# First batch's decays in two parts, corrections in one operation, and chunk magnitudes as powers of two

## The chip, the cores and the metric

The kernel runs on one core of a Trainium2 chip. Its engines are TensorE (PE, matrix multiply), VectorE (DVE), ScalarE (ACT), GpSimd (POOL) and SyncE (SP), each with its own queue of instructions, worked in order. The metric is the device time of one execution in microseconds. Times that belong to one profiled execution are counted from its first instruction.

## The reference

The layer takes q, k, v and a complex decay a (4 batches, 8 heads, 768 positions, 48 numbers a head), carries a state through the positions, and sends the result through two mixers:

```python
mag = np.sqrt(a_re * a_re + a_im * a_im)
scale = np.minimum(mag, 0.999) / (mag + 1e-06)
a_re_n, a_im_n = (a_re * scale, a_im * scale)
for t in range(S):
    ar, ai = (a_re_n[:, :, t, :, None], a_im_n[:, :, t, :, None])
    new_re = ar * S_re - ai * S_im
    new_im = ar * S_im + ai * S_re
    kv = np.einsum('bhd,bhe->bhde', k[:, :, t], v[:, :, t])
    S_re, S_im = (new_re + kv, new_im)
    y[:, :, t] = np.einsum('bhd,bhde->bhe', q[:, :, t], S_re)
# x: y with the heads side by side, 384 numbers a position
h = np.maximum(xt @ w_tok1, 0.0) @ w_tok2        # xt: positions last
u = x + h.transpose(0, 2, 1)
x = u + np.maximum(u @ w_ch1, 0.0) @ w_ch2
xn = (x - mu) / np.sqrt(var + 1e-06) * g_ln
out = x + np.maximum(xn @ w_ch1, 0.0) @ w_ch2    # second set of weights
```

## The kernel before

The recurrence is turned into products. The running product of the decays up to each position multiplies q, and its inverse multiplies k; within a chunk of 128 positions the result is then a masked matrix product, and a small scan over the six chunks carries the state. Four generators issue this, and a scheduler sets each engine's order from what they issue.

`gen_E` makes the decays and the products of one batch, on rows of 128 (head, number) pairs: 384 such rows are three row tiles, i = 0, 1, 2, each in two halves `hf` of 384 positions. It has four stages. **A** loads a into the tile `aj` (`load_a`), squares it (L202), and normalises it (L207 to L226). **The scan** (L228 to L230) multiplies 16 blocks of 24 columns one after the other, 15 complex steps (`cmul`) over all three row tiles at once. **L2** (L231 to L272) scans the 24 column ends in a tile `I`, takes the chunks' magnitudes by ScalarE (L248, L249) and a Newton step, and makes one correction for each column in the tile `C`. **C** (L273 to L343) goes by row tile and half: two products of `aj` with the correction (L295, L297, to `t`), a difference and a sum into `aj` (L299, L301), which read every third number; squares, logarithm and exponential for the inverse; the products with q and k (L328, L330); and DMAs on SP that put them into a tile `stk` for each head (L337, L338). Heads 0 and 1 lie in row tile 0; head 2 in 0 and 1; 3 and 4 in 1; 5 in 1 and 2; 6 and 7 in 2.

`gen_P` works one head on PE: transposes of k (L415), scores (L428) which VectorE masks (L433), state products (L455) and the chunk scan on VectorE (L456), the output (L475 to L487), and its split into two 16-bit halves `xh` and `xl` (L384). When the v of head 7 is loaded it also issues the second batch's three loads of a (L364 to L367). `gen_W` splits a weight tile that came as 64-bit numbers into two 16-bit halves by three operations on VectorE and one on ScalarE (L520 to L524); 4 token weights and 24 channel weights. `gen_M` is the two mixers: token products (L597 to L616), and hidden tiles (`relu_split`, L563 on ScalarE and L565 on VectorE), 198 in all.

In the first batch all loads are pieces of 4 runs of 192 numbers (L60). SP's queue holds, in order: the six loads of a, the constants, gl, q and k, weights, v, and then the transfers to `stk`. `gstat`, a product of gl with itself (L95), stands early in VectorE's queue.

Of the kernel before, what the change touches and what calls it, by code (L numbers as in the profile page):

```python
# [9 lines left out]
F32 = mybir.dt.float32  # L10
# [11 lines left out]
P = 128  # L22
# [14 lines left out]
def tile_kernel(ctx: ExitStack, tc: tile.TileContext, a_in, qk_in, v_in, aq2_in, v2_in, wt_in, wm1_in, wm2_in, w64_in, g_in, c_in, out):  # L37
# [16 lines left out]
    def steps(x, i, half):  # L54

        x = x.rearrange("p x (h i s) -> p (x h) i s", i=3, h=2)[:, :, i]
        return x if half is None else x[:, :, half * (HB // 2):(half + 1) * (HB // 2)]

    def load_a(b, i, half=None):
        nc.sync.dma_start(out=steps(aj, i, half), in_=steps(a_in[b], i, half))  # L60

    for half in range(2):
        for i in range(3):
            load_a(0, i, half)
# [123 lines left out]
    def gen_E():  # L188
# [3 lines left out]
        av = aj.rearrange("p x (j k r) -> p x j k r", j=6, k=KB)  # L192
        for b in range(B):
            rec[0] = b == 0
            for hf in range(2):
                for i in range(3):
                    ah = steps(aj, i, hf)
                    t = scratch(b, 2 * i + hf)
                    s4, s5, s6, s7 = (t[:, j * HB:(j + 1) * HB] for j in range(4))
                    g = wact.get(min(27, AG + (2 * i + hf) * AGS)) if b == 1 and AG >= 0 else None  # L200
                    with (tc.issue_after(g) if g is not None else ExitStack()):
                        A.activation(out=t[:, 0:2 * HB].rearrange("p (y s) -> p y s", y=4), in_=ah, func=AF.Square)  # L202
                    yield "wait"
                    if b < PNA:
                        nn = pe_sum(PNT, (eye, s4), (eye, s5))
                    else:
                        V.scalar_tensor_tensor(out=s4, in0=s4, scalar=TINY, in1=s5, op0=ALU.add, op1=ALU.add)  # L207
                        nn = s4
                    A.activation(out=s5, in_=nn, func=AF.Ln, bias=b_tiny if b < PNA else b_zero)
                    A.activation(out=s5, in_=s5, func=AF.Exp, scale=-0.5, bias=b_ln)  # L210
                    A.activation(out=s6, in_=s5, func=AF.Square, scale=1.0 / 0.4995,
                                 accum_out=rstat[:, 6 * b + 2 * i + hf:6 * b + 2 * i + hf + 1])
                    if b == 0:
                        V.tensor_scalar(out=s7, in0=s5, scalar1=-EPS / 0.4995, scalar2=1.0, op0=ALU.mult, op1=ALU.add)
                    else:
                        A.activation(out=s7, in_=s5, func=AF.Identity, scale=-EPS / 0.4995, bias=b_one)
                    yield 470
                    yield "wait"
                    V.scalar_tensor_tensor(out=s4, in0=nn, scalar=-1.0, in1=s6, op0=ALU.mult, op1=ALU.mult)
                    yield 470  # L220
                    V.scalar_tensor_tensor(out=s5, in0=s4, scalar=3.0, in1=s5, op0=ALU.add, op1=ALU.mult)
                    yield 470
                    V.scalar_tensor_tensor(out=s4, in0=s5, scalar=1.0, in1=s7, op0=ALU.min, op1=ALU.mult)
                    yield 470
                    ah = ah.rearrange("p (x h) s -> p x h s", x=2)
                    V.tensor_tensor(out=ah, in0=ah, in1=pair(s4.rearrange("p (h s) -> p h s", h=2)), op=ALU.mult)  # L226
                    yield 870
                for j in range(max(1, hf * KB // 2), (hf + 1) * KB // 2):  # L228
                    cmul(av[:, 0, :, j], av[:, 1, :, j], av[:, :, :, j], av[:, :, :, j - 1], [6, 24])
                    yield 1200  # L230
            yield "L2"  # L231
            NC3 = 3 * NCH
            I = ap.tile([P, 2, 6, 24], F32, tag="I", name="I")
            Iv = I.rearrange("p x (i h) r -> p x i h r", i=3)
            for h in range(2):
                V.tensor_copy(out=Iv[:, :, :, h], in_=av[:, :, 3 * h:3 * h + 3, KB - 1])
            yield 400
            for d in (3, 6, 12):
                cmul(I[:, 0, :, d:], I[:, 1, :, d:], I[:, :, :, d:], I[:, :, :, :24 - d], [6, 24 - d])
                yield 900  # L240
            ac = I[:, :, :, 21:24]
            sq = ap.tile([P, 2, NC3], F32, tag="sq", name="sq")
            st = ap.tile([P, 4, NC3], F32, tag="st", name="st")
            r0, r1, r2, dc = (st[:, j] for j in range(4))
            pc = pstat[:, b]
            V.tensor_tensor(out=sq.rearrange("p x (h c) -> p x h c", c=3), in0=ac, in1=ac, op=ALU.mult)
            V.scalar_tensor_tensor(out=pc, in0=sq[:, 0], scalar=TINY, in1=sq[:, 1], op0=ALU.add, op1=ALU.add)
            A.activation(out=r0, in_=pc, func=AF.Ln)  # L248
            A.activation(out=r0, in_=r0, func=AF.Exp, scale=-0.5)  # L249
            yield 300  # L250
# [23 lines left out]
            for i in range(3):  # L274
# [66 lines left out]
                if b and b + 1 < B:  # L341
                    load_a(b + 1, i)
# [810 lines left out]
```

## Time and profile before

| | us |
|---|---|
| runs | 962.79, 964.20, 966.58 (median 964.2) |
| span of the profiled execution | 960.0 |
| PE busy / VectorE busy / ScalarE busy | 816.3 / 746.6 / 495.8 |
| mean granted PE clock, share of full | 0.973 |

The page gives a span and not a whole time for the profiled execution; the median of the runs is 4.2 us above the span. Busy counts the time in which an engine worked on something, so PE's 816.3 us are 85% of the span and VectorE's 78%. A row of the time order gives start, length, engine, line, operation, what it writes and reads, shapes, count, and in brackets how long the engine sat idle before it and what ended that.

### The profile page before, as it was taken

Reading aid. Unit: us, or ns where it says so; the run is one execution under the profiler, and the core shown is the slowest. Engines: PE = TensorE matmul, PEld = TensorE weight load, DVE = VectorE, ACT = ScalarE, POOL = GpSimd, SP = SyncE. Lnnn points to the kernel's source line nnn. Section 1 sums busy time; section 2 is a strip of 40 time slices with the busy share of each in tenths; the row PEclk is TensorE's granted clock in tenths of the full one; section 3 lists DMA queues with packets and bytes.
Section 4 is the critical chain, followed back from the end, with each engine's and each line's share of the span. In section 5 each row is a group of like instructions: output and inputs, shape, how many; then the busy total and the mean of one; then the engine's idle time right before and its main releaser. Section 6 shows DMA issues by size and latency. Waiting matters only on the chain.

```text
span 960.0 us, 15755 instructions
## 1 busy us (share of the span) xinstructions
PE 816.3 (85%) x5738; PEld 559.3 (58%) x5738; DVE 746.6 (78%) x1535; ACT 495.8 (52%) x1367; POOL 57.9 (6%) x113
## 2 busy tenths in 40 slices
PE   0004998689989999999999989698999999999995
PEld 0004998446656777665666755465666666656563
DVE  6999976999999779998997999899676523264543
ACT  6004334743354559434869972465677534353642
POOL 0000011000101000002200000011000000011110
PEclk9999997799999979999999999999999999999998
DMA  8204587033414551116533110333120102356562
GB/s 286 99 33 122 155 275 282 7 132 132 156 52 131 151 171 37 65 33 159 129 103 89 32 62 29 98 103 104 43 64 26 50 2 91 122 171 218 189 219 91
DMA packets 47495, 108.28 MB, mean 113 GB/s; under 512 B 5808, under 2 KB 33072, under 8 KB 47408
## 3 DMA queue, kind: packets, MB, share of 16 engines
q1 hardware_dynamic: 39024, 61.57, 21.9%
q0 software_dynamic: 8384, 45.62, 14.0%
q8 instruction: 47, 0.77, 0.3%
q14 instruction: 40, 0.33, 0.1%
HBM read 77.20 MB, written 11.01 MB: 92 GB/s over the span
## 4 chain that ended last, share of the span: by engine, by line
PE 37%; DVE 18%; ACT 4%; DMA 2%; issue 2%; SPq 1%; DVEq 0%; ACTq 0%
PE m L555 11%; PE m L556 11%; PE m L557 11%; DVE t L175 5%; DVE aj L175 3%; DVE hid L565 2%; DVE p L175 1%; DMA stk<-t 1%; PE sc L428 1%; DVE qh L446 1%; DVE qk L175 1%; DVE U L456 1%; DVE r L433 1%; DVE hl L437 1%; PE tr L455 1%
## 5 line engine op out<-in xcount | busy, mean ns | idle before, releaser
L565 DVE SCALAR_TENSOR_TENSOR hid<-m,hid 128x384 f16<-128x384 f32 x198 | 109.1, 551 | 116.2 <-ACT hid L563 115.9
L555 PE MATMUL m<-u,w 128*128 128x384 f16 x576 | 188.4, 328 | 3.8 <-DVE u L615 3.4
L556 PE MATMUL m<-u,w 128*128 128x384 f16 x576 | 188.7, 328 | 1.1 <-DVE u L676 1.1
L557 PE MATMUL m<-u,w 128*128 128x384 f16 x576 | 188.7, 328 | 0.0
L563 ACT ACTIVATE hid<-m 128x384 f16<-128x384 f32 x198 | 96.1, 485 | 178.4 <-PE m L557 177.8
L556 PE MATMUL m<-hid,w 128*128 128x384 f16 x540 | 176.0, 326 | 10.7 <-DVE hid L565 10.3
L557 PE MATMUL m<-hid,w 128*128 128x384 f16 x540 | 176.0, 326 | 0.0
L557 PEld LDWEIGHTS <-w 128*128 128x128 f16 x1176 | 115.9, 99 | 89.7 <-issue 20.2
L556 PEld LDWEIGHTS <-w 128*128 128x128 f16 x1176 | 116.4, 99 | 76.8 <-issue 6.7
L555 PEld LDWEIGHTS <-w 128*128 128x128 f16 x1176 | 115.9, 99 | 75.6 <-issue 6.8
L555 PE MATMUL m<-hid,w 128*128 128x384 f16 x540 | 129.0, 327 | 3.2 <-ACT hid L563 2.7
L415 PE MATMUL tr<-cst,stk 96*128 96x96 f32 x125 | 17.0, 259 | 85.6 <-DMA stk<-qk 85.6
L175 DVE SCALAR_TENSOR_TENSOR t<-t 128x384 f32<-128x384 f32 x120 | 64.1, 548 | 17.5 <-ACT t L202 11.8
L415 PEld LDWEIGHTS tr<-cst,stk 96*128 96x128 f32 x125 | 14.2, 151 | 88.0 <-issue 86.2
L175 DVE TENSOR_TENSOR p<-aj 128x288 f32<-128x288 f32 x120 | 49.3, 449 | 0.8
L523 ACT ACTIVATE w<-raw 128x768 f16<-128x768 f32 x28 | 25.2, 899 | 45.1 <-DVE raw L521 42.8
L428 PE MATMUL sc<-stk 96*128 96x128 f32 x300 | 46.1, 291 | 0.2 <-DVE sT L433 0.2
L428 PEld LDWEIGHTS sc<-stk 96*128 96x128 f32 x300 | 41.8, 203 | 2.5 <-DVE sT L433 0.4
L175 DVE TENSOR_TENSOR t<-aj,I 128x768 f32<-128x768 f32 x40 | 36.0, 951 | 7.9 <-DMA stk<-t 7.0
L503 POOL DMA_DIRECT2D raw<-in_wm x48 | 25.9, 539 | 215.1 <-DVE w L524 107.0
L563 ACT ACTIVATION_READ_ACCUMULATOR hid<-m 128x1 f32 x198 | 38.6, 195 | 0.0
L536 ACT ACTIVATE sq<-sq 128x768 f16<-128x768 uint8 x28 | 23.6, 843 | 27.8 <-DVE sq L535 27.8
(273 smaller groups left out, 1650.9 us busy)
## 6 DMA issues: line engine op xcount, KB each, us to landing
raw<-in_wm POOLq DMA_DIRECT2D x48, 768.0 KB, 4.7
qk<-in_qk SPq DMA_DIRECT2D x23, 384.0 KB, 4.3
aj<-in_a SPq DMA_DIRECT2D x9, 768.0 KB, 6.6
stk<-t SPq DMA_DIRECT2D x40, 144.6 KB, 3.2
stk<-qk SPq DMA_DIRECT2D x40, 144.6 KB, 3.1
raw<-in_wt SPq DMA_DIRECT2D x6, 768.0 KB, 4.8
v<-in_v SPq DMA_DIRECT2D x32, 144.0 KB, 2.3
tokw<-tokw_d POOLq DMA_DIRECT2D x6, 768.0 KB, 4.6
```

The costliest lines, as they stand in the source:

```text
L175: r = getattr(nc.vector, n)(*a, **k)
L415: T.transpose(tr[:, c * 96:(c + 1) * 96], qc(c, 1), eye[0:96, 0:96])
L428: last = T.matmul(sc[:, (c % 3) * P:(c % 3 + 1) * P], qc(c, 1), qc(c, 0), start=True, stop=True)
L433: ev = V.tensor_tensor(out=sT[half], in0=sc[:, 0:3 * P].rearrange("p (c t) -> p c t", c=3), in1=pair(mask, 3), op=ALU.mult)
L503: (nc.sync if n < NSY else nc.gpsimd).dma_start(out=raw.bitcast(U8), in_=w_src[n].bitcast(U8)[:, 3:3 + 8 * S])
L523: wact[n] = A.activation(out=dst[:, :, 0], in_=w, func=AF.Copy, scale=WS).ins
L536: A.activation(out=t[:, HB:2 * HB].bitcast(F16), in_=bad_, func=AF.Copy, accum_out=wstat[:, n:n + 1])
L555: T.matmul(out_, wh, xh_, start=first, stop=False)
L556: T.matmul(out_, wh, xl_, start=False, stop=False)
L557: T.matmul(out_, wl, xh_, start=False, stop=last)
L563: A.activation(out=hl[:, 0], in_=p, func=AF.Relu, accum_out=hstat[:, n_h[0]:n_h[0] + 1])
L565: last[:] = [V.scalar_tensor_tensor(out=hl[:, 1], in0=p, scalar=0.0, in1=hl[:, 0], op0=ALU.max, op1=ALU.subtract).ins]
```

## The change

The decays of batch 0 are worked in two parts, `PARTS`: stages A, scan, L2 and C for row tiles 0 and 1, then for tile 2; other batches keep one part. The layout of a changes: a row tile's two halves lie side by side, and the 24 columns of a block go by chunk (three times 8), no longer with the chunk running fastest. The loads of batch 0 go by real and imaginary plane, twelve instead of six; the next batch's load of a row tile is issued as soon as that tile's C stage is issued, for batch 0 too, and no longer with a v. The chunk magnitude becomes a power of two, by bit operations on VectorE. The correction tile `Ct` holds a negated copy beside real and imaginary part, so that each of the two products makes terms that only need adding: one operation of 768 in place of two of 384. The four token weights are split only after the first part's scan, the first batch's part 2 is issued between the first heads with a budget `EB2`, and the program's scratch for software DMAs is set to 8192.

```diff
+        for x in range(2) if half is not None else (slice(0, 2),):
+            nc.sync.dma_start(out=o[:, x], in_=s[:, x])
+    for part in PARTS:
+        for half in range(2):
+            for i in part:
+                load_a(0, i, half)
...
+            for part in PARTS if b == 0 else ((0, 1, 2),):
+                for x in gen_A(b, part):
+                    yield x
+                for x in gen_L2(b, part, Ct, W, sq, st):
+                    yield x
+                yield "C"
+                for i in part:
+                    for x in gen_C(b, i, Ct, st, nxt_q):
+                        yield x
+                    if b + 1 < B:
+                        load_a(b + 1, i)
+                    yield ("done", b, i)
...
+            for j in range(max(1, hf * KB // 2), (hf + 1) * KB // 2):
+                cmul(av[:, 0, js, j], av[:, 1, js, j], av[:, :, js, j], av[:, :, js, j - 1], [n, 24])
+        fin["scan"] = e0[-1]
...
-            A.activation(out=r0, in_=pc, func=AF.Ln)
-            A.activation(out=r0, in_=r0, func=AF.Exp, scale=-0.5)
-            V.tensor_tensor(out=r1, in0=r0, in1=r0, op=ALU.mult)
-            V.scalar_tensor_tensor(out=r1, in0=pc, scalar=-0.5, in1=r1, op0=ALU.mult, op1=ALU.mult)
-            V.scalar_tensor_tensor(out=r2, in0=r1, scalar=1.5, in1=r0, op0=ALU.add, op1=ALU.mult)
-            V.tensor_tensor(out=dc, in0=pc, in1=r2, op=ALU.mult)
+        V.tensor_scalar(out=g.bitcast(U32), in0=pc.bitcast(U32), scalar1=1, scalar2=0x3F800000, op0=ALU.logical_shift_right, op1=ALU.bitwise_and)
+        V.tensor_scalar(out=dc.bitcast(U32), in0=g.bitcast(U32), scalar1=0x20000000, scalar2=None, op0=ALU.bitwise_or)
+        V.tensor_scalar(out=g.bitcast(U32), in0=dc.bitcast(U32), scalar1=0x7F800000, scalar2=None, op0=ALU.bitwise_xor)
...
+        V.tensor_copy(out=Iv[:, :, :, 0], in_=Wl)
+        A.activation(out=Il[:, 0], in_=Iv[:, 1], func=AF.Copy, scale=-1.0)
...
-                        V.tensor_tensor(out=t4[:, 0:2], in0=ah, in1=Cb[0], op=ALU.mult)
-                    V.tensor_tensor(out=t4[:, 2:4], in0=ah, in1=Cb[1], op=ALU.mult)
-                    V.tensor_tensor(out=am[:, 0], in0=tm[:, 0], in1=tm[:, 3], op=ALU.subtract)
-                    V.tensor_tensor(out=am[:, 1], in0=tm[:, 1], in1=tm[:, 2], op=ALU.add)
+                        for y in range(2):
+                            V.tensor_tensor(out=tp[y], in0=pair(ah[:, y]), in1=Ct[:, 1 - y:3 - y, j * 24:(j + 1) * 24].unsqueeze(2).to_broadcast([P, 2, KB, 24]), op=ALU.mult)
+                    V.tensor_tensor(out=an.rearrange("p x (c k n) -> p x c k n", c=3, k=KB), in0=ts[0], in1=ts[1], op=ALU.add)
...
-                if n == VA:
-                    with tc.issue_after(x.ins):
-                        for i in range(3):
-                            load_a(1, i)
...
+            with tc.issue_after(fin["scan"]):
+                split_w(hl, n)
...
         run_P()
+        if 2 <= st["e"] < 3:
+            run_E(EB2)
+    run_E(0, until=3)
...
+PARTS, EB2 = ((0, 1), (2,)), 4000
...
-    nc = _bacc.Bacc("TRN2", target_bir_lowering=False, num_devices=1)
+    nc = _bacc.Bacc("TRN2", target_bir_lowering=False, num_devices=1, dynamic_dma_scratch_size=8192)
```

Three places show how instructions move. The first is VectorE's queue at the end of the first batch's normalisation, around the first scan step (`p` from `aj`, then `aj` from `p`); `pad` and `raw` are a weight split, `w_100` and `w_106` one shared tile. Before:

```order
L175 SCALAR_TENSOR_TENSOR w_100<-w_100 128x384 x3
L175 SCALAR_TENSOR_TENSOR t<-t 128x384
L520 SCALAR_TENSOR_TENSOR pad<-raw 128x768
L175 TENSOR_TENSOR aj<-aj,w_100 128x4x192
L175 SCALAR_TENSOR_TENSOR w_100<-w_100 128x384 x2
L175 SCALAR_TENSOR_TENSOR t<-t 128x384
L521 SCALAR_TENSOR_TENSOR raw<-raw,pad 128x768
L175 TENSOR_TENSOR p<-aj 128x288 x2
L175 SCALAR_TENSOR_TENSOR w_100<-w_100 128x384 x2
L175 TENSOR_TENSOR aj<-aj,t 128x4x192
L520 SCALAR_TENSOR_TENSOR pad<-raw 128x768
L175 TENSOR_TENSOR aj<-p 128x6x24 x2
L524 SCALAR_TENSOR_TENSOR w_100<-raw,w_100 128x2x384
```

And now:

```order
L179 SCALAR_TENSOR_TENSOR w_106<-w_106 128x384
L179 TENSOR_TENSOR p<-aj 128x192 x2
L179 SCALAR_TENSOR_TENSOR w_106<-w_106 128x384
L179 TENSOR_TENSOR aj<-aj,t 128x2x2x192
L179 SCALAR_TENSOR_TENSOR w_106<-w_106 128x384 x2
L179 TENSOR_TENSOR aj<-p 128x4x24 x2
L179 SCALAR_TENSOR_TENSOR w_106<-w_106 128x384
L179 TENSOR_TENSOR aj<-aj,w_106 128x2x2x192
L179 SCALAR_TENSOR_TENSOR w_106<-w_106 128x384
L179 TENSOR_TENSOR p<-aj 128x192 x2
L179 SCALAR_TENSOR_TENSOR w_106<-w_106 128x384
L179 TENSOR_TENSOR aj<-aj,w_106 128x2x2x192
L179 TENSOR_TENSOR aj<-p 128x4x24 x2
```

The weight split is gone from here, and a scan step covers 4 blocks of columns where it covered 6. The second place is VectorE's queue where the corrections begin (`t`, `u` and the shared tile from `aj` and `I`). Before:

```order
L175 COPY I<-W 128x12x3
L175 TENSOR_TENSOR t<-aj,I 128x768 x4
L175 TENSOR_TENSOR u<-aj,I 128x768
L175 TENSOR_TENSOR w_100<-aj,I 128x768 x3
L175 MEMSET W 128x3 x2
L175 TENSOR_TENSOR aj<-t 128x384 x4
L175 SCALAR_TENSOR_TENSOR t<-t 128x384 x3
L175 TENSOR_TENSOR t<-qk,t 128x384
L175 SCALAR_TENSOR_TENSOR t<-t 128x384
L175 SCALAR_TENSOR_TENSOR qk<-t 128x384
L175 TENSOR_TENSOR t<-qk,t 128x384
L175 TENSOR_TENSOR t<-qk,aj 128x768
```

And now:

```order
L179 COPY I<-W 128x2x12
L179 TENSOR_TENSOR p<-aj 128x96 x2
L179 TENSOR_TENSOR t<-aj,I 128x2x16x24 x4
L179 TENSOR_TENSOR aj<-p 128x2x24 x2
L179 TENSOR_TENSOR aj<-t 128x2x384 x2
L179 TENSOR_TENSOR p<-aj 128x96 x2
L179 SCALAR_TENSOR_TENSOR t<-t 128x384
L179 TENSOR_TENSOR aj<-p 128x2x24 x2
L179 SCALAR_TENSOR_TENSOR t<-t 128x384
L179 TENSOR_TENSOR p<-aj 128x96 x2
L179 TENSOR_TENSOR aj<-p 128x2x24 x2
L179 SCALAR_TENSOR_TENSOR t<-t 128x384
```

The scan steps of row tile 2 (96 elements) stand between the corrections of row tile 0, the products of later tiles no longer stand ahead, and one operation of 768 takes the place of two of 384. The third place is VectorE's queue around the products of row tile 1 with q and k (`qk` from `qk` and `aj`; `r` and `U` are work of the heads). Before:

```order
L175 SCALAR_TENSOR_TENSOR w_100<-w_100 128x384
L456 SCALAR_TENSOR_TENSOR U<-m_614,dr 96x288
L175 TENSOR_TENSOR qk_105<-qk_105,aj 128x768
L175 TENSOR_TENSOR w_100<-aj,I 128x768
L433 TENSOR_TENSOR r<-sc,cst 128x384
L175 SCALAR_TENSOR_TENSOR w_100<-w_100 128x384
L520 SCALAR_TENSOR_TENSOR pad<-raw 128x768
L175 TENSOR_TENSOR aj<-w_100 128x384 x2
L175 TENSOR_TENSOR w_100<-qk_105,w_100 128x384
L521 SCALAR_TENSOR_TENSOR raw<-raw,pad 128x768
L384 SCALAR_TENSOR_TENSOR xl<-m_594,xh 128x6x48
L175 SCALAR_TENSOR_TENSOR qk_105<-w_100 128x384
```

And now:

```order
L179 TENSOR_TENSOR w_106<-qk_111,w_106 128x384
L179 TENSOR_TENSOR aj<-p 128x2x24 x2
L179 TENSOR_TENSOR qk<-qk,aj 128x768
L179 TENSOR_TENSOR aj<-aj,t 128x2x2x192
L179 SCALAR_TENSOR_TENSOR qk_111<-w_106 128x384
L179 TENSOR_TENSOR p<-aj 128x96 x2
L179 TENSOR_TENSOR w_106<-qk_111,aj 128x768
L179 TENSOR_TENSOR aj<-p 128x2x24 x2
L530 SCALAR_TENSOR_TENSOR pad<-raw 128x768
L179 TENSOR_TENSOR qk_111<-qk_111,aj 128x768
L179 COPY I<-aj 128x2x48
L531 SCALAR_TENSOR_TENSOR raw<-raw,pad 128x768
```

Between the two products of row tile 1 now stand the end of row tile 2's scan and the normalisation of the second batch's first piece (`aj` from `aj` and `t`).

## Rows read from the trace of the kernel before

**Rows 1.** The page's 40 slices: busy tenths of two engines

```profile
PE   0004998689989999999999989698999999999995
...
DVE  6999976999999779998997999899676523264543
```

**Rows 2.** Busy time by stretch: start:end length, engines (count), clock, DMA, GB/s

```profile
122.56:170.87 48.31, 43.06 (x271) 40.48 (x271) 35.10 (x53) 20.82 (x49) 5.92 (x11) 0.82 0.78 274
170.87:199.59 28.72, 16.05 (x104) 10.06 (x104) 28.72 (x51) 20.79 (x51) 1.08 (x2) 0.82 0.10 30
199.59:279.70 80.11, 76.69 (x453) 45.20 (x453) 75.70 (x174) 33.50 (x86) 5.93 (x14) 0.98 0.37 123
279.70:410.00 130.30, 127.34 (x951) 93.85 (x949) 116.12 (x238) 76.20 (x215) 5.97 (x10) 0.96 0.37 109
410.00:501.00 91.00, 85.96 (x617) 55.68 (x616) 85.72 (x182) 49.43 (x141) 11.01 (x12) 1.00 0.37 100
501.00:615.80 114.80, 102.67 (x851) 68.88 (x850) 104.47 (x248) 83.25 (x246) 1.76 (x6) 1.00 0.21 66
615.80:675.00 59.20, 54.83 (x412) 36.17 (x411) 54.41 (x93) 33.37 (x92) 5.75 (x8) 0.97 0.38 102
```

**Rows 3.** VectorE in order of time, 0 to 95 us: start, length, instruction

```profile
12.22 0.16 DVE L95 TENSOR_TENSOR gstat<-gl 128x3 f32<-128x3 f32 x1 [0.76 <-DMA gl<-in_g]
...
52.69 0.82 DVE L175 TENSOR_TENSOR p<-aj 128x288 f32<-128x288 f32 x2
...
54.11 0.38 DVE L175 COPY I<-aj 128x144 f32<-128x144 f32 x2
...
57.03 0.53 DVE L175 TENSOR_TENSOR p<-I 128x144 f32<-128x144 f32 x2
...
58.00 0.20 DVE L175 TENSOR_TENSOR sq<-I 128x36 f32<-128x36 f32 x1
...
78.85 0.95 DVE L175 TENSOR_TENSOR qk<-qk,aj 128x768 f32<-128x768 f32 x1
```

**Rows 4.** The matrix engine in order of time, its first work

```profile
83.87 0.71 PE L415 MATMUL tr<-cst,stk 96*128 96x96 f32 x3 [83.87 <-DMA stk<-qk]
```

**Rows 5.** VectorE in order of time, 95 to 240 us

```profile
98.82 0.93 DVE L175 TENSOR_TENSOR qk<-qk,aj 128x768 f32<-128x768 f32 x1
...
121.61 0.95 DVE L175 TENSOR_TENSOR u<-u,aj 128x768 f32<-128x768 f32 x1
...
170.87 0.45 DVE L384 SCALAR_TENSOR_TENSOR xl<-m,xh 128x288 f16<-128x288 f32 x1
...
199.59 0.54 DVE L565 SCALAR_TENSOR_TENSOR hid<-m,hid 128x384 f16<-128x384 f32 x1
```

**Rows 6.** Busy time by stretch of the hidden tiles' line alone, first stretch

```profile
199.59:279.70 80.11, 13.71 (x26) 0.98 0.37 123
```

**Rows 7.** VectorE by line and shape: busy us, mean ns, idle before

```profile
L175 DVE SCALAR_TENSOR_TENSOR t<-t 128x384 f32<-128x384 f32 x120 | 64.1, 548 | 17.5 <-ACT t L202 11.8 <-ACT t L319 3.7 <-ACT t L303 0.9
L520 DVE SCALAR_TENSOR_TENSOR pad<-raw 128x768 uint8<-128x768 uint8 x28 | 28.6, 1023 | 7.2 <-DMA raw<-in_wm 6.8 <-DMA raw<-in_wt 0.3
L521 DVE SCALAR_TENSOR_TENSOR raw<-raw,pad 128x768 uint32<-128x768 uint32 x28 | 26.6, 951 | 0.1
L524 DVE SCALAR_TENSOR_TENSOR w<-raw,w 128x768 f16<-128x768 f32 x28 | 26.6, 950 | 1.6 <-ACT w L523 1.5
L175 DVE TENSOR_TENSOR aj<-t 128x384 f32<-128x384 f32 x40 | 25.0, 674 | 0.0
```

**Rows 8.** SP's DMA issues in order of time, two pieces

```profile
0.89 4.17 SPq L60 DMA_DIRECT2D aj<-in_a  x6
...
144.12 2.08 SPq L60 DMA_DIRECT2D aj<-in_a  x3
```

**Rows 9.** The page's DMA issues: count, KB each, us to landing

```profile
aj<-in_a SPq DMA_DIRECT2D x9, 768.0 KB, 6.6
```

**Rows 10.** Waits of the matrix engine, 600 to 675 us: total, times, longest

```profile
PE m L555 <- DVE u L615: 6.7, 3, 3.1
```

More of the change, by code (lines that the diff above doesn't have):

```diff
@@ L54, in steps @@
     def steps(x, i, half):
-        x = x.rearrange("p x (h i s) -> p (x h) i s", i=3, h=2)[:, :, i]
-        return x if half is None else x[:, :, half * (HB // 2):(half + 1) * (HB // 2)]
+        if half is None:
+            return x[:, :, i * S:(i + 1) * S]
+        return x.rearrange("p x (i h s) -> p x i h s", i=3, h=2)[:, :, i, :, half * (HB // 2):(half + 1) * (HB // 2)]
     def load_a(b, i, half=None):
-        nc.sync.dma_start(out=steps(aj, i, half), in_=steps(a_in[b], i, half))
-    for half in range(2):
-        for i in range(3):
-            load_a(0, i, half)
+        o, s = steps(aj, i, half), steps(a_in[b], i, half)
+        for x in range(2) if half is not None else (slice(0, 2),):
[4 more added lines that the diff above has]
+                load_a(0, i, half)
     cst = cp.tile([P, 2 * P + 3], F32, name="cst")
@@ L191, in gen_E @@
         load_w(1)
-        av = aj.rearrange("p x (j k r) -> p x j k r", j=6, k=KB)
         for b in range(B):
             rec[0] = b == 0
[L195 to L247, printed above, removed]
-            A.activation(out=r0, in_=pc, func=AF.Ln)
-            A.activation(out=r0, in_=r0, func=AF.Exp, scale=-0.5)
-            yield 300
-            yield "wait"
-            V.tensor_tensor(out=r1, in0=r0, in1=r0, op=ALU.mult)
-            V.scalar_tensor_tensor(out=r1, in0=pc, scalar=-0.5, in1=r1, op0=ALU.mult, op1=ALU.mult)
-            V.scalar_tensor_tensor(out=r2, in0=r1, scalar=1.5, in1=r0, op0=ALU.add, op1=ALU.mult)
-            V.tensor_tensor(out=dc, in0=pc, in1=r2, op=ALU.mult)
-            V.memset(dc.rearrange("p (i c) -> p i c", i=3)[:, :, NCH - 1:], 0.0)
@@ L257, in gen_E @@
+            Ct = ap.tile([P, 3, 6 * 24], F32, tag="I", name="I")
             W = ap.tile([P, 2, 3, NCH], F32, tag="W", name="W")
+            sq = ap.tile([P, 2, 3 * NCH], F32, tag="sq", name="sq")
+            st = ap.tile([P, 2, 3 * NCH], F32, tag="st", name="st")
             V.memset(W[:, 0, :, 0:1], 1.0)
             V.memset(W[:, 1, :, 0:1], 0.0)
[L260 removed]
@@ L276, in gen_E, with gen_C @@
+    def gen_C(b, i, Ct, st, nxt_q):
+        V = Rec()
+        dc = st[:, 0]
+        yield ("need", b * H + ((i + 1) * P - 1) // D + 1 - NSTK if b else 0)
+        if True:
+            if True:
                 for hf in range(2):
@@ L340, in gen_E @@
                     yield 870
-                if b and b + 1 < B:
-                    load_a(b + 1, i)
-                yield ("done", b, i)
     def warm(n, w, after=None):
@@ L361, in load_v @@
                     t = ap.tile([P, NCH, D], F32, tag="v", name="v", bufs=NV)
-                x = nc.sync.dma_start(out=t, in_=v_in[heads[n]])
+                nc.sync.dma_start(out=t, in_=v_in[heads[n]])
                 vt[heads[n]] = t
-                if n == VA:
-                    with tc.issue_after(x.ins):
-                        for i in range(3):
-                            load_a(1, i)
         loaded = [0]
```

100 lines of the change are left out of this document (72 added, 28 removed).

## The prediction

> **What bounds the kernel now.** I read the 40 slices first: the matrix engine does nothing in the first three and a half slices and is then nearly full to the end, while VectorE is full from the second slice to about the 28th [rows 1]. So the end is the moment at which the matrix engine gets going, plus its own work, plus what VectorE makes it wait. The table by stretch says where [rows 2]. After 615.8 us VectorE has time to spare; from 199.6 to 615.8 us it is 89 to 95% busy and the matrix engine 89 to 98%: two engines that both run close to full, so that a microsecond added to VectorE there is partly paid. From 122.6 to 170.9 us neither is full (35.1 and 43.1 of 48.3 us).
>
> Then the order of time on VectorE. The 15 scan steps of the first batch cost 1.42 us each (52.69 to 54.11), the first finished product of q and k ends at 79.8, and the first transpose starts 4.1 us later at 83.87 [rows 3, 4]. The last product of that batch ends at 122.5, the eighth head's low half is taken out at 170.87, and the first hidden tile at 199.59 [rows 5]. From that hidden tile on I cut the span where the 26th, 51st, 76th, 101st and 116th of the 198 hidden tiles start, because both kernels pass the same marks [rows 6]. VectorE's work between two marks is summed in each kernel's own order of instructions, each at the start-to-start spacing of its shape in the trace.
>
> **Part by part: the start.** The stem of the argument is VectorE's queue up to the first product.
> - Two weight splits stood in it (three instructions each, 1.023, 0.951 and 0.950 us [rows 7], 2.65 us as they follow each other); now none does: 5.3 us less.
> - The 15 scan steps work 4 instead of 6 columns. A step of 288/144 elements takes 1.42 us and one of 144/72 takes 0.97 (57.03 to 58.00) [rows 3]. On that line 192/96 costs 1.12 and 96/48 costs 0.82. So 15 times 0.30 = 4.5 us leave the path, but the third tile pays 15 times 0.82 = 12.3 us afterwards: 7.8 us more in total.
> - The second-level scan, chunk magnitudes (no round trip to ScalarE) and corrections up to the first product: 25.7 us before (54.11 to 79.8), summed now 23.8 with five interleaved steps of the third tile (4.1 us) in it. 1.9 us less, bounds 0 and 3: the waits for ScalarE may stay.
> - The six loads become twelve. Six took 4.17 us to issue [rows 8]; six more delay what is behind them by as much, and VectorE stands at gl's arrival at 12.22 [rows 3]. Loss between 0 and 4.2 us; I take 0.7, since gl then no longer queues behind as much data.
>
> First product at 79.8 - 5.3 - 4.5 - 1.9 + 0.7 = about 69 us, first transpose at 73: 11 us earlier.
>
> **What gives it back.** After that product VectorE's queue now holds ten of the third tile's scan steps (8.2 us), its second-level scan (5.5), two normalisations of the second batch (each four operations of 0.47 and one of 0.87: 2.75 us), whose loads now leave as soon as a tile of the first batch is done instead of at 144.12 [rows 8], and products of the second tile that stood ahead of it. Against that, fewer weight splits. My sum from the first product to the second tile's two products is 26.9 and 31.7 us: 96 and 101 us (99.7 for the second before [rows 5]), to the third tile's last 63.8 us and about 2 of waits for ScalarE: 135 us, against 122.5 [rows 5]. On ScalarE the second batch's first square now stands ahead of the second tile's squares and of head 1's copy of k; it waits for a load that leaves behind twelve stk transfers, near 77 us, and takes about 6.6 [rows 9]. Until about 85 us head 1 stands on the matrix engine; that is idle time ahead of head 2 either way. So heads 0 and 1 start 11 us early, heads 2 to 4 hardly at all, and the last three have their data 12 us late. Before, the matrix engine was behind: it needed (170.87 - 83.87) / 8 = 10.9 us a head, with half a token product in it. Now it has worked off heads 0 to 4 when the third tile comes, and needs about 31 us for the last three from 136: 167 us against 170.87. Behind the eighth head's low half stand 26.4 us of VectorE work before the first hidden tile (28.7 measured before), so this comes at about 194, 5.6 us earlier; bounds 188 and 201. They are from the clock: its mean in this stretch was 0.82 [rows 2], between the levels of 1.2 and 2.4 GHz, and the three heads take 31 x 0.82 = 25 us at the higher level throughout and 31 / 0.82 = 38 if gaps on the matrix engine keep it down longer than before.
>
> **The merged corrections.** Two subtractions/additions of 384 elements (674 ns each) become one operation of 768. Their operands were read at every third number; a plain 384 takes 548 [rows 7], a plain product of 768 takes 0.95 us [rows 3]. The new one reads runs of eight numbers. It costs between 0.95 us (no penalty) and 1.35 (two of the strided kind); I take 0.95, as the scan's operations on runs of 24 show no penalty. That is 0.33 us of spacing, 24 times: 8 us, six of them in batches 1 to 3.
> The Trainium skill's "SBUF — State Buffer" (Door 1: The DMA port swizzle) says that successive accesses within one 16-byte line run at full bandwidth, so that fp32 may be strided by up to four numbers. This case's row disagrees on the stride of three, which costs 126 ns on 384 elements; eight in a row are two full lines, and by the rule they would cost nothing, as I take them.
> The negated copy of the corrections on ScalarE hides behind the two products that don't need it. Magnitudes by bit operations save about 0.5 us a batch. [...]
>
> **The middle.** VectorE's work between the marks, before and now: to the first hidden tile 171.1 and 163.5 us; then 77.3 and 83.7, 115.1 and 127.2, 85.1 and 90.2, 102.5 and 102.8, 53.6 and 43.8. The change puts off ten weight splits beyond the first hidden tile (8 are done there, 18 before) and brings the later batches' decays forward: E of the last batch ends four hidden tiles earlier. With the stretches' lengths of 80.1, 130.3, 91.0, 114.8 and 59.2 us [rows 2] I take the larger of the two engines' needs: 84.5, 131.3, 92, 113.8 and 53, that is +4.4, +1, +1, -1 and -6 = -0.6 us. The -6 rests on the stretch where the matrix engine waited 6.7 us for VectorE's u operations [rows 10]. If every extra microsecond were paid and nothing returned at the end, it would be +10; if the first stretches absorbed it, -7.
>
> **Sum.** -5.6 - 0.6 = -6.2 us. The profiled span is 960.0; the median of the runs is 4.2 us above it, which I take as what lies around the span. 964.2 - 6.2 = 958 us.
>
> **Rivals.**
> - *VectorE pays for it all (slower).* Place: the stretch from the first hidden tile to the 76th. If the last three heads take the whole 38 us and the first hidden tile comes at 201, nothing is gained at the start, and the deferred ten splits (26.5 us) with the 12.1 us more in the second stretch push VectorE's need (301 us) over the 301.4 us that these three stretches have. Price: +2 at the start, +8 in the middle: 974 us. It decides as soon as VectorE idles less than 3% there. For it: 95% busy already. Against it: 14 us of idle in the second stretch [rows 2].
> - *The early start survives.* If the idle 13 us from 122.6 to 170.9 are filled by the third tile and the second batch, the matrix engine keeps 11 us, and the middle gives 2 more: 951 us. Against it: the weights' raw loads are behind the third tile in the queue, so that VectorE has no splits to fill with.
> - *Nothing moves.* The gain of heads 0 and 1 is lost at head 2, the last three heads end when they did, and what the merged corrections save falls on stretches where the matrix engine is the bound: 964 us. For it: 98% matrix busy in the second stretch.
>
> **Numbers.** Forecast 0.50 (951 to 966 us; about 0.32 faster, 0.18 same), slower rival 0.22 (0.20 slower, 0.02 same), early start 0.14 (faster), nothing moves 0.14 (0.12 same, 0.02 slower). Half a percent (4.8 us) is about what can be told from no change. Faster 0.46, same 0.32, slower 0.22. The range for 8 in 10 reaches into both side cases: 946 to 973 us.
>
> **What would show it.** First transpose at 70 to 76 us; a gap on the matrix engine before head 2 that ends near 100; third tile's last product at 132 to 139; first hidden tile near 194; the merged operation at 0.95 us; last decay product four hidden tiles earlier. The forecast is wrong if the first hidden tile comes after 200, or if the first three stretches after it take more than 310 us.

## The result, and the profile after

The changed kernel takes 972.3 us (median of 5, 968.4 to 973.7) against 963.8 (962.2 to 966.6) for the kernel before, run beside it: a ratio of 1.0105, interval [1.0070, 1.0141]. It is slower by 1%; 958 was forecast. The profiled execution took 972.28 us, its span is 970.6 (before 960.0).

The page's 40 slices and the heads of its chain, changed kernel, as [rows 1]:

```profile
PE   0018989699988899999889999799999999999996
...
DVE  6999957999997788997979999988675523264543
...
PE 40%; DVE 28%; DMA 11%; issue 10%; ACT 6%; SPq 4%; POOL 0%; DVEq 0%; POOLq 0%; ACTq 0%
```

The matrix engine now starts in the third slice, and the end is later all the same. The chain that ended last has 11% of transfers in it; in the kernel before these were 2%.

The start first: VectorE in order of time, the matrix engine's first work, and VectorE up to the first hidden tile, changed kernel, as [rows 3 to 5]:

```profile
65.04 0.95 DVE L179 TENSOR_TENSOR qk<-qk,aj 128x768 f32<-128x768 f32 x1
...
94.52 0.95 DVE L179 TENSOR_TENSOR qk<-qk,aj 128x768 f32<-128x768 f32 x1
...
127.45 0.96 DVE L179 TENSOR_TENSOR u<-u,aj 128x768 f32<-128x768 f32 x1
...
165.17 0.46 DVE L394 SCALAR_TENSOR_TENSOR xl<-m,xh 128x288 f16<-128x288 f32 x1 [1.01 <-ACT xh L393]
...
192.73 0.55 DVE L576 SCALAR_TENSOR_TENSOR hid<-m,hid 128x384 f16<-128x384 f32 x1
```

```profile
69.80 0.71 PE L425 MATMUL tr<-cst,stk 96*128 96x96 f32 x3 [69.80 <-DMA stk<-qk]
```

The first product comes 13.8 us earlier than before, the first transpose 14.1, the eighth head 5.7 and the first hidden tile 6.9. So the start gave about what was forecast. Then the busy time between the same hidden tiles as in [rows 2]: from the 1st to the 26th, 51st, 76th, 101st and 116th, changed kernel:

```profile
192.70:275.30 82.60, 77.88 (x468) 45.87 (x467) 81.04 (x171) 35.44 (x86) 5.97 (x13) 1.00 0.33 110
275.30:419.70 144.40, 132.67 (x935) 95.44 (x935) 128.17 (x249) 82.50 (x220) 10.74 (x15) 0.92 0.41 125
419.70:525.90 106.20, 96.70 (x727) 63.14 (x725) 92.18 (x188) 63.64 (x183) 6.84 (x12) 0.97 0.34 95
525.90:633.10 107.20, 99.23 (x761) 64.91 (x759) 103.28 (x241) 70.72 (x209) 2.88 (x8) 0.98 0.23 71
633.10:687.90 54.80, 51.28 (x395) 33.66 (x392) 45.03 (x76) 30.86 (x86) 7.71 (x6) 1.00 0.35 93
```

| hidden tiles | before, us | forecast: VectorE's need, length | after: VectorE busy, length |
|---|---|---|---|
| 1 to 26 | 80.1 | 83.7, 84.5 | 81.0, 82.6 |
| 26 to 51 | 130.3 | 127.2, 131.3 | 128.2, 144.4 |
| 51 to 76 | 91.0 | 90.2, 92 | 92.2, 106.2 |
| 76 to 101 | 114.8 | 102.8, 113.8 | 103.3, 107.2 |
| 101 to 116 | 59.2 | 43.8, 53 | 45.0, 54.8 |

VectorE's work was forecast to within 3 us in every stretch. The lengths of the second and third were not: they are 13.1 and 14.2 us longer than forecast (the fourth 6.6 us shorter), and neither engine is full there. VectorE stands idle for 16.2 and 14.0 us, the matrix engine for 11.7 and 9.5. Something new is waited for. What VectorE waits for from transfers, changed kernel (total, times, longest):

```profile
DVE t L179 <- DMA stk<-t: 11.8, 7, 3.3
DVE t L179 <- DMA stk<-qk: 4.6, 2, 2.8
...
DVE aj L179 <- DMA aj<-in_a: 2.8, 2, 2.7
```

The last row is the clue, small as it is. In the kernel before no operation that writes `aj` with the corrections waited for a load. Here is one in order of time, in the second batch: VectorE, and SP's load beside it, changed kernel:

```profile
297.76 1.81 DVE L179 TENSOR_TENSOR t<-aj,I 128x768 f32<-128x768 f32 x2
...
305.08 1.83 DVE L179 TENSOR_TENSOR t<-aj,I 128x768 f32<-128x768 f32 x2 [1.87 <-DMA stk<-qk]
...
310.69 0.96 DVE L179 TENSOR_TENSOR aj<-t 128x768 f32<-128x768 f32 x1 [2.66 <-DMA aj<-in_a]
```

```profile
301.52 0.66 SPq L63 DMA_DIRECT2D aj<-in_a  x1
```

The products that the merged operation adds up end at 299.6; it starts at 310.7, when the third batch's load into row tile 0, issued at 301.52, has landed. It writes row tile 1. The columns are disjoint, and it waits nevertheless. VectorE's list of instructions says it (number, line, operation, what it waits for; DMAHW is a transfer, DVE_49 is VectorE's own earlier work), so the wait was written when the list was made:

```
611 L179 TENSOR_TENSOR aj<-t 128x2x384 [waits DMAHW2_49]
612 L179 TENSOR_TENSOR aj<-t 128x2x384 [waits DVE_49]
```

Five of the merged operations have such a wait: one in the first batch, two in the second, two in the third; none in the kernel before. There each of the two operations wrote one plane (384 numbers); the merged one writes the real and the imaginary plane at once (2x384), and the load covers both planes too, with runs of 768. The first of the five is at 78.23; its load was issued at 72.79 and landed 4.8 us later:

```profile
65.91 1.82 DVE L179 TENSOR_TENSOR u<-aj,I 128x768 f32<-128x768 f32 x2
...
78.23 0.95 DVE L179 TENSOR_TENSOR aj<-u 128x768 f32<-128x768 f32 x1
```

That row names no idle time: other work stands in the 10.5 us between the products and the operation, in an order of instructions that was made with the wait known. So the cost need not be idle time at the waiting instruction. Where it appears is further on: in e5 below, which lacks the wait, the second batch's corrections start at 253.43 us, here at 271.38.

### The profile page after: what moved, and what is told of

It reads as the page before. It is cut to its first block, busy times and chain, and to the rows that moved or that the text cites. A ratio compares the mean times of both kernels' runs of the same rounds, so it can differ in the third digit from the quotient of the medians.

```text
span 970.6 us, 15833 instructions
## 1 busy us (share of the span) xinstructions
PE 834.6 (86%) x5738; PEld 570.6 (59%) x5738; DVE 744.1 (77%) x1597; ACT 496.8 (51%) x1364; POOL 59.6 (6%) x113
## 3 DMA queue, kind: packets, MB, share of 16 engines
q0 software_dynamic: 8384, 45.62, 14.2%
## 4 chain that ended last, share of the span: by engine, by line
PE 40%; DVE 28%; DMA 11%; issue 10%; ACT 6%; SPq 4%; POOL 0%; DVEq 0%; POOLq 0%; ACTq 0%
PE m L566 11%; PE m L567 11%; PE m L568 11%; DVE t L179 6%; DVE aj L179 4%; DVE p L179 4%; DMA stk<-t 3%; DMA stk<-qk 2%; DMA raw<-in_wm 2%; DMA aj<-in_a 2%; DVE hid L576 2%; PE sc L438 2%; SPq L355 2%; SPq L356 1%; DVE qk L179 1%
## 5 line engine op out<-in xcount | busy, mean ns | idle before, releaser
L179 DVE TENSOR_TENSOR p<-aj 128x288 f32<-128x288 f32 (+2 forms) x150 | 52.7, 392 | 0.8
L179 DVE TENSOR_TENSOR t<-aj,I 128x768 f32<-128x768 f32 x40 | 36.4, 953 | 16.5 <-DMA stk<-t 11.8
L533 ACT ACTIVATE w<-raw 128x768 f16<-128x768 f32 x28 | 25.4, 906 | 30.0 <-DVE raw L531 29.8
```

The source lines that it names most:

```text
L179: r = getattr(nc.vector, n)(*a, **k)
L533: wact[n] = A.activation(out=dst[:, :, 0], in_=w, func=AF.Copy, scale=WS).ins
```

## The experiments

The kernel before, run beside each of them, took 960.9 to 962.3 us (963.8 above), so ratios to it are what is compared. Theory A was that the first batch's late third tile and the weight splits put off by it cost the time, theory B that the later batches or the corrections do. Both stood before I had read the row of `aj` and in_a rightly.

**e1_whole**: the first batch in one part again.
```diff
-PARTS, EB2 = ((0, 1), (2,)), 4000
+PARTS, EB2 = ((0, 1, 2),), -1
```


> The first batch's three row tiles are worked in one part again; merged corrections, magnitudes by powers of two, the early loads of the second batch and the gated token splits stay. Theory A (the third tile, 12 us later, leaves the matrix engine short of heads, and puts off weight splits that then meet the second batch's decays): the first hidden tile comes at 196 to 201 us, 16 to 19 weight splits are done before it, the stretch from hidden tile 36 to 41 takes 35 to 40 us instead of 50.6, and the median is 955 to 962 us. Theory B (the second batch's decays or the corrections' new form bring the loss, whatever the first batch does): the stretch 36 to 41 still takes over 45 us and the median is 967 to 973 us.

965.3 us, ratio 1.0049 [1.0017, 1.0080]; hidden tile 1 at 193.6 us, 36 at 317.0, 41 at 367.2: the stretch takes 50.2 us as in the changed kernel. Better by half a per cent, but not where theory A has it; the time lies between the two ranges, and the stretch is theory B's.

**e2_early_splits**: the two token splits ungated.
```diff
-            with tc.issue_after(fin["scan"]):
-                split_w(hl, n)
+            split_w(hl, n)
```


> The first two token-weight splits may run ahead of the first batch's scan again, all else as in the changed kernel. Theory A: the first product comes about 5 us later (70 us instead of 65), the splits' debt at the first hidden tile is two smaller (10 instead of 8 done), the third tile is as late as in the changed kernel: 966 to 972 us. Theory D (the loss is the debt of weight splits alone, whatever the third tile does): each split paid early takes 2.65 us from the stretch before hidden tile 36: 962 to 966 us.

971.5 us, 1.0106 [1.0072, 1.0139]: no difference to the changed kernel. The first hidden tile came 5.9 us earlier (186.8), hidden tile 41 at 362.5 (363.0): nothing of it was left. Theory D falls.

**e3_late_a**: the second batch's loads at the eighth head's v again.
```diff
-                    if b + 1 < B:
+                    if b and b + 1 < B:
...
+                if n == VA:
+                    with tc.issue_after(x.ins):
+                        for i in range(3):
+                            load_a(1, i)
```


> The second batch's decays are loaded at the eighth head's v again, after the first batch, all else as in the changed kernel. Theory A: the third tile is 3 to 6 us earlier, since two normalisations of the second batch (2.75 us each) and their squares on ScalarE no longer stand ahead of it; three or four more weight splits fit before the first hidden tile; the second batch's decays come later by as much: 964 to 971 us. Theory L (the early loads and the decays they start are what hurts): the stretch 36 to 41 takes under 40 us and the median is 955 to 962 us.

969.3 us, 1.0113 [1.0065, 1.0161]. The first hidden tile came at 176.6, 16 us ahead of the changed kernel's, and hidden tile 41 at 364.8; the stretch from 36 to 41, under 40 us by theory L, takes 66.7. Theory L falls.

**e4_corr_only**: the three edits above together, so that only corrections, magnitudes and layout are left.


> One part, ungated token splits and late loads of the second batch: of the change only the merged corrections, the magnitudes and the new layout are left. Theory A: VectorE has about 8 + 2 us less to do and nothing else moves: first hidden tile at 196 to 199 us, 957 to 962 us. Theory B: 967 us or more, since the corrections' form or the second batch's order brings the loss.

974.7 us, 1.0160 [1.0121, 1.0199]: the slowest. Theory A falls with it: without any split the loss is larger. In all five kernels hidden tile 41 comes between 362.5 and 367.2 us, wherever the first hidden tile was (176.6 to 193.6). That points at something that runs beside the mixer and sets that tile: the second batch's decays and heads. In the kernel before it came at 359.7. What the five have in common is the corrections, magnitudes and layout, and with them the wait. In e3 and e4, whose second batch is loaded after the first, only the second and third batch's operations wait.

The next four take the wait away by loading other pieces: with the load's runs as long as the merged operation's (384 numbers), the two are no longer taken to overlap, and the list has `[waits DVE_49]` at all of them. Two things come with that edit: six loads of 384 KB in place of three of 768 KB (median 4.6 us to landing in e5, 5.0 in the changed kernel), and a new order of all queues. No run has the small loads with the wait, or the large ones without it.
```diff
+        if half is None:
+            for j in (2 * i, 2 * i + 1):
+                nc.sync.dma_start(out=aj[:, :, j * HB:(j + 1) * HB], in_=a_in[b][:, :, j * HB:(j + 1) * HB])
+            return
```

**e5_half_loads**: the changed kernel with that.


> The changed kernel with one edit: the next batch's decays are loaded as six half tiles (columns of one correction each) instead of three whole tiles. Theory F (the first correction of row tiles 1 and 2 waits for the load of the next batch into the tile before it, though the columns are disjoint; that holds the second and third batch's decays back by about 9 us each time): in the second batch's third half the merged operation follows its products by 2 to 5 us instead of 11.1, the stage from the first product with the corrections to the last q and k product takes 70 to 77 us instead of 86 in the second batch and 70 to 80 instead of 91 in the third; hidden tile 41 comes at 345 to 355 us, the median is 955 to 963 us. Theory A or the clock (the deferred splits or the matrix engine's lower level bring the loss, the wait of 2.8 us in all is covered): hidden tile 41 stays at 360 to 366 us, 968 to 973 us.

960.4 us, 1.0004 [0.9988, 1.0021]: the loss of 1.0105 is gone. Hidden tile 41 comes at 357.5 (363.0), 76 at 508.6 (525.9). The merged operations, VectorE, e5_half_loads, first, second and third batch:

```profile
64.74 1.82 DVE L183 TENSOR_TENSOR u<-aj,I 128x768 f32<-128x768 f32 x2
...
67.68 0.95 DVE L183 TENSOR_TENSOR aj<-u 128x768 f32<-128x768 f32 x1
...
253.43 1.80 DVE L183 TENSOR_TENSOR t<-aj,I 128x768 f32<-128x768 f32 x2
...
286.82 1.80 DVE L183 TENSOR_TENSOR t<-aj,I 128x768 f32<-128x768 f32 x2
...
292.95 0.94 DVE L183 TENSOR_TENSOR aj<-t 128x768 f32<-128x768 f32 x1
...
438.11 1.83 DVE L183 TENSOR_TENSOR t<-aj,I 128x768 f32<-128x768 f32 x2 [1.90 <-DMA stk<-t]
...
440.32 0.94 DVE L183 TENSOR_TENSOR aj<-t 128x768 f32<-128x768 f32 x1
```

1.1, 4.3 and 0.4 us after the products (10.5, 11.1 and 10.5 in the changed kernel). The third batch's stage takes 77 us (91), as expected. Two of the finer expectations missed: the second batch's stage still takes 86 us, but it starts at 253 instead of 271, and hidden tile 41 is 2.5 us later than the range that was given. The chain's head is again like that of the kernel before, DMA at 4%:

```profile
PE 37%; DVE 16%; DMA 4%; ACT 4%; issue 2%; SPq 2%; DVEq 0%; ACTq 0%
```

It is no measure of the time, though: the slow e8 below has 4% too, and e6, the fastest, has 7%.

**e6_whole_half_loads**: e1_whole with half loads.


> The first batch in one part, and the next batch's decays loaded as six half tiles. Theory F: the same gain as in the split kernel, 965 less 8 to 14 us: 951 to 957 us. Theory A or the clock: no more than 3 us from 965.

949.0 us, 0.9876 [0.9846, 0.9907]: 1.2% faster than the kernel before, the best version. In one part the wait shows in the first batch. VectorE, e1_whole, then e6_whole_half_loads:

```profile
73.36 1.82 DVE L179 TENSOR_TENSOR u<-aj,I 128x768 f32<-128x768 f32 x2
...
84.79 0.96 DVE L179 TENSOR_TENSOR aj<-u 128x768 f32<-128x768 f32 x1 [1.15 <-DMA aj<-in_a]
...
126.17 0.96 DVE L179 TENSOR_TENSOR u<-u,aj 128x768 f32<-128x768 f32 x1
```

```profile
73.63 1.82 DVE L183 TENSOR_TENSOR u<-aj,I 128x768 f32<-128x768 f32 x2
...
76.23 0.95 DVE L183 TENSOR_TENSOR aj<-u 128x768 f32<-128x768 f32 x1
...
115.01 0.94 DVE L183 TENSOR_TENSOR u<-u,aj 128x768 f32<-128x768 f32 x1
...
241.43 2.71 DVE L183 TENSOR_TENSOR t<-aj,I 128x768 f32<-128x768 f32 x3
```

The first batch's decays end 11.2 us earlier. e1_whole's corrections in the second batch start at 263.56, these 22 us earlier.

**e7_corr_half_loads**: e4_corr_only with half loads.


> Of the change only the corrections, magnitudes and layout (one part, ungated splits, late load of the second batch), and the loads as six half tiles. Theory F: this is what the merged corrections are worth by themselves: 956 to 962 us, and hidden tile 41 at 345 to 352 us instead of 366. Theory A or the clock: 970 to 976 us.

963.6 us, 1.0021 [0.9996, 1.0046], from 1.0160: the wait's price again, though by the median a little above the range given, and hidden tile 41 only at 359.8 (345 to 352 expected). The first hidden tile came at 183.2, 16.4 us ahead of the kernel before, and nothing of that is left at the 41st.

**e8_late_a_half_loads**: e3_late_a with half loads.


> The changed kernel with the second batch's decays loaded at the eighth head's v and all loads as half tiles. Its first hidden tile came at 176.6 us, 16 us ahead of the changed kernel's, and nothing of it was left at hidden tile 41. Theory F: part of the early start survives, hidden tile 41 at 340 to 352 us, 945 to 958 us. Rival (the second batch's decays come too late for the mixers' early start, whatever they wait for): hidden tile 41 stays above 358 us, 962 us or more.

971.6 us, 1.0132 [1.0091, 1.0173]: no gain, against theory F's number. Hidden tile 41 at 360.5 and the time are the rival's. Its second batch's corrections start at 270.96 us, and in e3_late_a at 271.64. But a late start alone is not the reason: in e4 and e7 they start as late (274.90 and 276.43), and there the wait's going is worth 1.4%. In e8's profile, of the fastest of its six executions, hidden tile 76 still comes 8.1 us earlier than in e3 (511.0, 519.1), and tile 101 is 0.8 us later (625.4, 624.6). What takes the gain back between them is not shown.

**e9_ungated**, **e10_late_a**: e6 with the token splits ungated (as in e2), and e6 with the second batch's late loads (as in e3).


> One part, half loads (949.0 us), and the first two token-weight splits may run ahead of the first batch's scan again. If the gate is what makes the one-part kernel fast: the first product 5 us later and 954 to 960 us. If it is the early load of the second batch: 948 to 952 us.

> One part, half loads, gate kept, and the second batch's decays loaded at the eighth head's v. If the early load is what makes the one-part kernel fast (hidden tile 41 is set by the second batch's decays, and their start sets these): the corrections' stage of the second batch starts at 260 us or later instead of 241.4, hidden tile 41 at 356 us or later instead of 349.6, 957 to 964 us. If the gate: 948 to 953 us.

950.6 us, 0.9882 [0.9851, 0.9913], and 961.6 us, 0.9989 [0.9959, 1.0019]. The gate is worth nothing that can be told, the early load 1.1%. The corrections of the second batch, VectorE, e10_late_a (241.43 in e6):

```profile
278.74 2.71 DVE L183 TENSOR_TENSOR t<-aj,I 128x768 f32<-128x768 f32 x3
```

**e11_wait_in_first**: e6 with whole-tile loads, and so the wait, in the first batch alone (the half loads under `half is None and b > 1`).


> One part, and only the second batch's loads, which are issued during the first batch, as whole tiles: the merged operation waits for a load in the first batch alone. If the wait costs where the trace shows it longest (second and third batch): 949 to 952 us, hidden tile 41 near 350. If a third or more of the 16 us is paid at the start (hidden tile 1 came at 193.6 with all waits and at 186.3 with none): hidden tile 1 at 191 us or later and 954 to 960 us.

963.5 us, 1.0016 [0.9986, 1.0046], above both ranges. With the wait in the first batch alone 1.4 of the 1.7% between e6 and e1 are paid; its merged operation waits there until 85.19:

```profile
85.19 0.96 DVE L183 TENSOR_TENSOR aj<-u 128x768 f32<-128x768 f32 x1 [1.27 <-DMA aj<-in_a]
```

**e12_eb**: e6 with more of the second batch's decays early (`EB0=500` to `EB0=1500`).


> One part, half loads, and three times as much of the second batch's decays written between two steps of the first twelve of the mixer (a budget of 1500 instead of 500). If hidden tile 41 is set by the second batch's decays and not by the mixer's start: these end 3 to 8 us earlier, the first hidden tiles come later, hidden tile 41 at 342 to 348 us, 942 to 948 us. If VectorE has no room there, the weight splits are what comes late: 949 to 955 us.

951.1 us, 0.9876 [0.9847, 0.9905]: the same as e6. That stage starts at 238.97, only 2.5 us earlier, but hidden tile 41 comes at 341.2, 8.4 us ahead of e6. At the 76th it is 2.2 us behind (503.3, 501.1). So a gain at tile 41 is not yet a gain at the end. Whether earlier decays would help further stays open.

**e13_split_wait_first**, **e14_split_wait_later**: e5 with the wait in the first batch alone (`b > 1`), and in the second and third alone (`b == 1`).


> The changed kernel (two parts) with whole-tile loads only for the second batch, so that the merged operation waits for a load in the first batch alone. In one part that alone cost 14.5 of 16 us. If it does so here: 969 to 974 us, and the second batch's stage with the corrections starts near 271 us. If the third tile's own steps cover the wait in the first batch (its last product came at 125.6 us with and without it): 958 to 963 us, and that stage starts near 253 us.

> The changed kernel with whole-tile loads only for the third and fourth batch: the merged operation waits in the second and third batch alone. If the first batch's wait carries the price: 959 to 963 us. If the later ones do (the trace of the changed kernel shows the merged operations 11 to 13 us behind their products there): 968 to 973 us and hidden tile 76 at 520 us or later instead of 508.6.

964.8 us, 1.0037 [1.0013, 1.0062], and 964.7 us, 1.0028 [1.0004, 1.0052]. Both lie between the ranges given. Neither place alone carries it: 0.3% and 0.2% above e5, and 1.0% with both. Corrections of the second batch start at 269.16 in e13 and 254.94 in e14, so the first batch's wait is what delays that start. How it does so is open: the first batch's last product (126.80) and the first hidden tile (190.5) are no later in e13 than in e5 (127.77, 191.4).

**e15_third_on_demand**: e5 with the third tile written only when a head asks for it.
```diff
-PARTS, EB2 = ((0, 1), (2,)), 4000
+PARTS, EB2 = ((0, 1), (2,)), -1
```


> The changed kernel with half loads (960.4 us), and the first batch's third tile written only when a head asks for it, not a budget of 4000 after each of the first heads' steps. If the split's price against one part (949.0) is that the third tile comes too late for the heads: its last product after 127 us and 962 to 968 us. If the price is VectorE's own longer work (7.7 us more in all), where the third tile stands in it matters little: 958 to 963 us.

960.1 us, 0.9978 [0.9955, 1.0002]: as e5. The budget moved the last product only by 0.5 us (127.77 to 128.28), so this tells little of the tile's place. What does tell is VectorE's busy time: 744.0 us in e5 and 735.7 in e6, 8.3 more, and e5's span is 8.0 us longer (the medians are 11.4 apart). The prediction had 7.8 us for the steps of the third tile. The sizes fit a split that costs what it adds; no run shows it, and the third tile's last product, 12.8 us later in e5 than in e6, is a rival.

## Why the prediction was wrong

**Start: right in the sum, partly by luck.** -5.6 us forecast, -6.9 measured at the first hidden tile. The first transpose came at 69.8 (73 forecast, range 70 to 76: just missed, early), the second tile's products ended at 90.9 and 95.5 (96 and 101), the third tile's last at 128.4 (135, range 132 to 139: missed, early), the gap ahead of head 2 ends at 93.8 (100). From the third tile's last product to the eighth head's low half it took 36.8 us where 31 were forecast. So a third tile 6.6 us early and three heads 5.8 us long cancelled. The last batch's last product comes after hidden tile 111 instead of 115: four earlier, as forecast.

**The merged operation: right as an operation.** 20 rows of 949 ns replace 40 of 674 [rows 7] on `t`. A plain product of 768 takes 0.95 us too [rows 3], so runs of eight show no price:

```profile
L179 DVE TENSOR_TENSOR aj<-t 128x768 f32<-128x768 f32 x20 | 18.4, 949 | 2.8 <-DMA aj<-in_a 2.8
```

The Trainium skill's "SBUF — State Buffer" (Door 1: The DMA port swizzle) lets fp32 be strided by up to four numbers without a price. The row agrees for runs of eight; for single numbers three apart the row of before, 674 against 548 ns, still speaks against it.

**The failed step is the one on the merged corrections and the layout under them.** It said of them only what they take from VectorE, "8 us, six of them in batches 1 to 3". The operation's wait for a load was in no term, nor in the price of the early loads, whose sentence asked what stands behind them on ScalarE and never who waits for their landing. VectorE's list of the changed kernel showed the five waits, and the prediction used that list for its order alone. With the wait gone the time falls by 1.0%, 1.7% and 1.4% in three pairs of kernels (e5, e6, e7), and not in the fourth (e8). That the wait brings the loss here is shown by e5 with the rows of the merged operation, but for what the smaller loads do by themselves (0.4 us less to landing). By which path it reaches the end is not shown: its places don't add up in the two-part kernel (e13, e14), e8 gains nothing, and each edit makes a new order of all queues, which no run varies by itself.

**A second error in the middle term.** It took each stretch as the larger of two engines' needs. From the first to the 76th hidden tile (busy rows of before, the changed kernel and e5, whole stretch):

```profile
199.59:501.00 301.41, 289.99 (x2017) 194.73 (x2017) 277.54 (x590) 159.13 (x441) 22.91 (x36) 0.98 0.37 110
```

```profile
192.70:525.90 333.20, 307.26 (x2128) 204.45 (x2127) 301.39 (x606) 181.58 (x489) 23.55 (x40) 0.95 0.37 112
```

```profile
191.40:508.60 317.20, 298.37 (x2084) 199.64 (x2084) 292.98 (x591) 175.47 (x470) 25.23 (x38) 0.97 0.39 116
```

VectorE idles 23.9 us of it before, 31.8 in the changed kernel and 24.2 in e5. Without the wait those 24 us of idle time are as long as before, and by this one comparison all of the 15.4 us more work (292.98 - 277.54) is paid: the stretch is 15.8 us longer, where I had charged 4.4 + 1 + 1 = 6.4. In spans: start -6.9, these stretches +31.8, given back behind them -12.5, in all +12.4 to the last hidden tile. Forecast: -5.6, +6.4, -7. Of the 25.4 us by which the middle was missed, e5 puts 9.4 on idle time that was not filled and 16 on the wait. Some of that 16 comes back behind the 76th hidden tile: e5 has -8.2 at the start, +15.8, and -7.1 behind, and the two kernels' last hidden tiles are 11.8 us apart.

**The rivals.** "VectorE pays for it all" had nearly the time (974) and the place, and its need of 301 us is what VectorE worked (301.39). But its late first hidden tile (201) did not come, and it was to decide when VectorE idles less than 3% there, and it idled 9.5%: 8 of its 32 us are the wait's. "The early start survives" falls with hidden tile 41, which came at 363.0 (359.7 before). "Nothing moves" is, by coincidence, what the change does without the wait (1.0004). The condition for a wrong forecast that was named, over 310 us in the first three stretches, is what happened: 333.2.

**Parts of the change, by the runs:** corrections, magnitudes and layout without the wait 1.0021 (e7), with gate and early load 0.9876 (e6), with the split 1.0004 (e5), with the wait 1.0105. The early load is the gain, the split and the wait are the losses. The 8 us of the merged corrections are in VectorE's busy time (737.7 us in e7, 746.6 before), and the time does not fall by them. The smaller scratch shows no price in the loads that use it: the weights' software loads land after 4.6 us (4.7 before). The Trainium skill's "DMA: Bandwidth & Descriptors" (Rules for kernel authors) says to issue a transfer early and to wait on it late. e6 against e10 agrees with its first half by 1.1%; the changed kernel broke the second without a line of code that says so, and e5 shows that at 1.0%.

## What to carry to other kernels

After a change of layout, read which instructions wait for which transfers in the new list before summing any duration: a write that is taken to overlap a load can wait for it although the columns are disjoint, and the wait can show as little idle time because other work is ordered into it; the distance from the last product to the operation showed it here (10.5 us, 1.1 without the wait). Don't count idle time as room in a stretch in which two engines are each over 90% busy: here work added to one of them was paid in full. And when a gain at the start is gone at one later point wherever the start was, look for the chain that sets that point, then test the end of the kernel as well: in e12 that point came 8 us earlier and the time stayed.

## What the runs showed of the hardware

The matrix engine's granted clock did not decide here. From 140 to 192 us it was at the lower of the two levels (1.2 GHz) most of the time in e5 and at the higher (2.4 GHz) in e15, which do nearly the same work there (busy rows of that stretch, e5, then e15):

```profile
140.00:192.00 52.00, 42.23 (x231) 34.00 (x231) 50.59 (x92) 31.30 (x72) 7.00 (x13) 0.65 0.52 180
```

```profile
140.00:192.00 52.00, 43.00 (x238) 35.13 (x238) 50.35 (x91) 31.08 (x72) 7.00 (x13) 0.97 0.54 180
```

From 140 to 172 us it was 0.50 in e5 and 1.00 in e15. The same matmuls have the same mean length there, by a profile in which their ends are modelled (e5, then e15):

```profile
L501 PE MATMUL m<-U,w 96*128 96x48 f32 x30 | 9.4, 410 | 0.7 <-DVE U L470 0.7
```

```profile
L501 PE MATMUL m<-U,w 96*128 96x48 f32 x30 | 9.4, 410 | 0.0
```

The first hidden tile came at 191.4 and 191.6, and the two kernels took 960.4 and 960.1 us. e5's own twelve executions took 958.4 to 962.0 us at mean clocks from 0.957 to 0.982; the four at 0.978 and above have 958.4, 960.5, 961.3 and 962.0. So the recorded level cost nothing that can be seen. Whether these matmuls don't need the clock, or the record of the level is off in one kernel, the rows can't tell. The prediction scaled the last three heads by it, 25 to 38 us "from the clock". From the third tile's last product to the eighth head's low half it took 39.1 us in e5 at 0.50 and 38.7 in e15 at 1.00, and 36.8 in the changed kernel at 0.59, so that scaling does not hold.
